# A chunked recurrence with a soft mixture of experts: Grams one step earlier, a new order of all instructions, and stores in half columns

## The chip, the cores and the metric

The kernel runs on one core of a Trainium2 chip. The metric is the time of one execution in device microseconds, the median of three runs. A core has five instruction streams that the profile names PE (TensorE; its weight loads have a row of their own, PEld), DVE (VectorE), ACT (ScalarE), POOL (GpSimd) and SP (SyncE, which here issues the data transfers). Everything is float32, but for the last products in fp32r.

## The reference

For 4 batches and 8 heads a state of 40 x 40 runs through 768 steps; then 3072 tokens of 320 values go through a soft mixture of 8 experts with 4 slots each.

```
for t in range(768):
    y[t]  = r[t] @ state
    Sa    = state @ a[t]
    state = state * w[t] - outer(Sa, b[t]) + outer(v[t], k[t])
x = y, as 3072 tokens x 320
logits = x @ phi                                   # 3072 x 32 slots
d = softmax(logits over tokens);  slot_in = d.T @ x
slot_out[e] = relu(slot_in[e] @ w1[e]) @ w2[e]     # 320 -> 1024 -> 320
out = softmax(logits over slots) @ slot_out
```

## The kernel before

The 768 steps are cut into 12 stages of 64, and a stage into two halves of 32 (q = 0, 1). The 8 heads of one batch go in groups of 3, 3 and 2 (120, 120 and 80 channels), times 4 batches: 12 groups.

For every stage there is work that does not depend on the state: running products of the decay w (scan_s, scan_k, scan_c: scans of 128 x 390 on VectorE and the products with k, b and a), a block-diagonal form of a (bda_at, ScalarE), and four Grams (gram, one for each batch): the products of k and b with a, 128 x 512 in one PSUM bank. Of a Gram, two 32-row parts go to the triangular systems (lls, two copies), and the rest is multiplied by a mask into SBUF (mls, VectorE). The systems of two stages are solved together (solve_in, 30 pairs of products and sums in solve_step on VectorE or GpSimd, solve_out): each of those steps needs the one before.

The chain is what the state runs through, stage by stage and half by half: chain_v (the part of v, 32 products of 32 x 40 columns, from mls), chain_a (the part of the state), chain_e (a copy to SBUF), chain_u (U, 32 products with the solved systems), six copies of U, and chain_s (the new state). Between these stand the output of the stage before (y_ut, y_sd, y_p, y_y), the transposes for later stages (kbtok, ctok_of) and the slots' online softmax (slots_a to slots_e). After the last stage come W1 (first), W2 (so), the combination of the slots' results (sr, s4) and the output: 24 products of 128 x 320, each copied from PSUM, and 12 stores of 256 x 320.

The program first records all operations (Plan.record) and only then issues them (Plan.emit). What comes when is written out in three strings: ORDER has two characters for each operation and is the order of the whole program, so each engine gets its own subsequence; ENGINE chooses ScalarE or VectorE for the copies marked `either`, and VectorE or GpSimd for the steps marked `both`; BANKS chooses a PSUM bank for every tenancy. Engines wait on each other by semaphores for data, and PACE holds transfers back when too many bytes are under way. All operations are issued from one helper line, L912 in the profile.

The order in which operations are recorded (the numbers in ORDER count them) is given by the loop over the stages, which records the Grams of stage st + 3 and the preparation of stage st + 4 behind the chain of stage st. The lines to which the change refers most:

```
nc.vector.tensor_tensor(mls[st][b][0:96], gr[0:96], mask_g[0:96]..., ALU.mult)
up = [bank(f"ups{st}"), bank(f"upt{st}")]
grams(st + 3)
run(*solve_items(st // 2 + 1))
nc.sync.dma_start(out[r].rearrange("(k p) c -> p k c", p=128), o2)
```

Of the kernel before, what the change touches and what calls it, by code (L numbers as in the profile page):

```python
# [14 lines left out]
MEM = 5560  # L15

B, H, S, D = 4, 8, 768, 40
C = 64
# [22 lines left out]
    "%:%9&,%k%p%n%l&R'[#,&O%m%o']'_%r%?%;%q&<&W&2%s%t%v'`'a'b'c'd%u&L&6&>%x&;&X&[%w&*%y&$%z%}%{&Y&%&.(N&#(L%|&Z&]"
    "&^&M&_&N&`(M&a&c&d'e'f&z'g'h&b'i'j'k&e&f&|'''l&9&g'm'%(O&A'n&='.'o&?&B&{'p&h&i&l&o&j&m&k&}'q'r&@'J's&D't'O&G"
    "'L'#&y'&(F(J'$'('F'u'D(G(K&s'v'w'x&C&n'K'y'z&H'{'+'-&v','/(H&p(I&F&t')&E&u'*'G&K(q&q'E&J(o(u&w(w'M(r(n(p(s)%"
    ")'(}&I&x)()&'8'9':(v'|'}(#($(%(&&r'@'B(''N(('Q'4()'R'T(x'5(y'U(t(*'6)^'S'<'7'A'H)_(z'V*`*f'^(+(,(-(.(/(0'X*c"
    "'P*6'C(1(2'?*a(3*4(|*b)$'Y'I(P';(4(5(6*d(7(8(9(:*7*e(Q*g*h)Y'W)))5(;(<(S)1)-'=)Z'>*j*5(=)*)T(>*k(?(A(D(B(C(@"
    "*l*i(T*m(R)7)6)3)/(E).)2(X*n)+)=(U(V(W(Z([*{)4(Y({(]*t*u*|)0)>(^(b'Z)9)U(`(_)[)8+#(a(d)#):);),(h+$+%+&(k(c*p"
    ")W(e+'+(+)(i)<)V+*(l(j(m)X*+(f(g)])`)a)b)c++)d)f)h)e)g)j+,+-+.)S*q)?)@*}*r)B*))A)i)C)E*%)k+/*#+f+l)l)D+g+0+n"
    ")m+1+2**+3)G+e*&*$*'+4+5)K)p+j)J+6)q)s)F+7+8)o*L)H*,)r*(*-+9)I)O)Q)P)N)R*N)n*O*.)w)L*Q*M)z*J+m+h)M*K*T){+k*D"
    "*E+:*P)|+;+<+i*8*R+=*U*/*1*3)}*S*@*B*0*X+o,3)x)y,5,9*2,;+>,4,6,7*W*<+?+@+A+B+C*A*C*H+D*V+E*Z*:*>,<*Y-U*]*G)t"
    "+F,:,=+G,8,o)u)v*I*s*;*[*F-S,X,]*9,Y+H,>.$.*,y+I+J.'+K+L+M+N+O,^,t.%+P+Q+R+S+T+U.&-V*=.(+p.)+q+V+W+X+Y+Z+[+]"  # L50
    "+^.+.,*^-T+s,L,N,Z,T,H..+_,M*?+`,z,P+t,[,U./*o,V,J,I.0+w,R,Q+v.A+u+x+r,C,B,?,@,A+z.B.-.C+{+y.D+|,F,O.1,}.:+}"
    ",2-$-#,K.E,W,&,{,u,$,%,#,),G,,.F,(.2.G,',w*_,|,/,v,S.H,_,D,x-D.3.I.J,*.K,-,+,0.9,.,1-%-B-'-(-H,E-J-.-+-,-&-)"
    "-E.L.M.N.O-*-/.P,a,`+b,e--.Q,b.R,p.S+c+a,d,q-0-C-I.T.U,s-F,c-1+d,f,g,i##,k-2-4.V.W.X.Y-6,h-7.5.;/f-K-l-L-3-5"
    "/.,j.6-G.Z.7/h.[-o-8-n-O.]/g-;-p-N-m,r.^-P._.`-M,m-Q,n-R/i->///4-s,l-t-h/,/--A-i-9-d/2-[.a-</5.b.c-q/3-j/0-W"
    "-g-^-e-=/1-f/S-:.d-r.e/T-u-k/V.f-v.g.h/].i.j.k.l-Y/U-x/W/Z/X-w-?-z0u-y/[0w0x-@-`0v0C.m-X/^.4/_0A/z-{-_-].n.o"
    ".p.q0#.r.s/Y-Z-b.#0D/`1G1D.t1J-a.u/|.v-}-|1E1H/61F.8/7.w.x1I-c.y.z/v.{.|.}/#/$/}/%/r/&/{/9/:1K/80$/a0&0B/<1L"
    "/;/x/t/w/=/b0(/c/>/A/@/s/n1N/+1O/)/(/'0+/y/B/C/*/j/?1P/u0%0;1M/p1Z1Q/D/E0?*v/G/k/q/l/e/F0'/o1b/I0E/P/M0@0)/m"
    "/H0=/J0>1U0<1c1R/N1e1f1g/K0f/Q1S/R/d/L1h1i1j1k1l1m0d/O0j0F1n0G0H0I0g0l1V0O0J0M0e0h0K1o0L0N0*1W0P0,0/0Q0-1p1Y"
    "1q1r1s0k08050607090m0i010R0n0S2N1t0.0X000U0V0T1415121u0W170]1T2L2O0`131v2J0o1w2K162H1[180Y0:3)2I1x2M0^1y0_3'"
    "2P3*3(1z0r0a1{0b0q0p0t1;2s2Q5<2y1>1<1|1}2#2w0c5=3A1=0s2q2t101?2x2r0304021@1&0y1*112u0Z1'0{0[0}1)1(1+4-1:1,0|"  # L60
    "1d1C1B1#2$2%2&2'2(2)2*2+1A2,2z1-2v2{1X5K3?4+192|45424/2-4.2.2/20212223241.3@370z40412p43443=1/463+3947333/2G"
    "4,3>3T2R25262728292S1%2:2;.<3B2<2=2}2>3-381]1$352?34313U302@2A2B492C4:2D2E3,2U3;4;2F4L4M4N2V4<3<3R483#2Y2Z2W"
    "2X2T3$2^2[3P2]3S524=3&3.4O4P4Q2_4R2`4S3:2d2c4>2b4T2f4D4U4V4W3L4X2a2j2e2m3N3Q2g534?4Y3C3M3O3u4Z4E4[3w2n4]4^5F"
    "2h323J4_4`4a3}2o3{2k2l2i3%4b3V3W3Y3X5P4c364d3Z3v3_3^3]3x3y3[4e3`5G3b5U3H3c3|5Y4f3a4g4h4i4j5Q3d3h3f3g3e3j3i3G"
    "4F4k3z4#4l4m3K3I4n4o5H555W4p4q574$3q3n4r4s4t4u5V4v4@4w4x4y4z4{5R5S3F4|3E3D3k4}3o5?5Z5M56545>3l5T4%5#5L5X3t5["
    "4'4&4(4*5z5{5$5|3m5}3r6%3p5N5O7*5I5:6'6&5;585%5&5'5(5)5*5+5,5-5J3s4)6#5^6(6$5.5/505]645@7+5_6)515`655b6*6`6c"
# [293 lines left out]
def rwkv_softmoe(ctx, tc, kb, aa, ww, rr, vv, vt, consts, phi, w1, w2, out):  # L360
# [8 lines left out]
    cs_t = cst.tile([128, 419], F32, name="cs_t")
    mask_g = cs_t[:, 0:64]  # L370
    mask_p = cs_t[:, 64:128]
    ident = cs_t[:, 128:256]
    sel, jj = cs_t[:, 259:291], cs_t[:, 291:419]
# [835 lines left out]
```

## Time and profile before

| | us |
|---|---|
| median of 3 runs (lowest, highest) | 381.95 (381.11, 383.08) |
| the profiled execution | 381.42 |
| its span | 379.7 |
| PE busy, PEld busy | 320.9, 280.4 |
| DVE busy | 304.7 |
| ACT busy | 211.5 |
| POOL busy | 114.8 |

Mean granted TensorE clock over the span: 0.936 of full speed. Data moved: 162 GB/s over the span.

The span is from the first instruction to the last, and the time of the execution has 1.7 us around it. Busy times of different engines overlap, so they do not add up; which of them holds up the end differs from stretch to stretch. An fp32 product appears as two matmul rows and two load rows, so counts in the trace are twice those in the code.

### The profile page before, as it was taken

The page shows a single profiled execution, that of the slowest core. Times are in us where ns is not written, and L with a number is a line of the kernel's source. Part 1 is how long each engine was busy: PE and PEld are TensorE (multiplying, and loading weights), DVE is VectorE, ACT ScalarE, POOL GpSimd, SP SyncE. Part 2 cuts the span into 40 slices and gives each one's busy share as a digit, 9 for nine tenths or more (in the row PEclk, how much of TensorE's full clock was granted, in tenths as well). Part 3 has the DMA queues.
Part 4 walks back from the last instruction along what each step waited for, and adds up shares of the span by engine and source line. Part 5 has one row for each costly group of instructions (what it writes and reads, how often), then busy time and mean ns, then how long its engine had stood idle before and what let it go on. Part 6 is the DMA issues. An engine that isn't in the chain of part 4 may idle for free.

```text
span 379.7 us, 15848 instructions
## 1 busy us (share of the span) xinstructions
PE 320.9 (85%) x6889; PEld 280.4 (74%) x6889; DVE 304.7 (80%) x660; ACT 211.5 (56%) x490; POOL 114.8 (30%) x220
## 2 busy tenths in 40 slices
...
GB/s 260 303 241 154 36 13 254 38 101 79 105 194 102 154 57 198 179 40 60 196 129 133 156 154 177 250 234 225 154 245 174 236 137 214 214 283 279 3 124 294
DMA packets 32798, 62.45 MB, mean 164 GB/s; under 512 B 3768, under 2 KB 18232, under 8 KB 32728
## 3 DMA queue, kind: packets, MB, share of 16 engines
...
q8 instruction: 54, 0.88, 1.0%
...
HBM read 57.49 MB, written 3.93 MB: 162 GB/s over the span
## 4 chain that ended last, share of the span: by engine, by line
PE 70%; DVE 10%; ACT 7%; issue 7%; DMA 1%; POOL 0%; ACTq 0%; DVEq 0%; POOLq 0%
PE ps L912 70%; DVE wt L912 7%; ACT wt L912 6%; DVE ps L912 1%; DVE mem L912 1%; DMA wt<-in_kb_dram 1%; ACT old L912 1%; ACT mid L912 0%; ACT mem L912 0%; ACT old_r L912 0%; POOL wt L912 0%; DVE slx L912 0%; DVE sls L912 0%; DVE mid L912 0%; ACTq L1205 0%
## 5 line engine op out<-in xcount | busy, mean ns | idle before, releaser
L912 PE MATMUL ps<-wt,wt 96*32 96x40 f32 (+7 forms) x2872 | 147.2, 240 | 14.8 <-ACT wt L912 7.2
L912 PEld LDWEIGHTS ps<-wt,wt 96*32 96x32 f32 (+7 forms) x2872 | 135.0, 134 | 22.8 <-issue 10.0
L912 POOL TENSOR_TENSOR wt<-wt 128x130 f32<-128x130 f32 (+14 forms) x194 | 96.1, 496 | 98.7 <-DVE wt L912 65.0
L912 ACT COPY wt<-ps 128x320 f32<-128x320 f32 (+3 forms) x120 | 53.5, 478 | 70.0 <-PE ps L912 56.8
L912 ACT ACTIVATE wt<-ps 32x256 f32<-32x256 f32 (+1 forms) x168 | 66.9, 399 | 27.8 <-PE ps L912 21.0
L912 PE MATMUL ps<-wt,mem 128*64 128x40 f32 (+4 forms) x1056 | 79.4, 264 | 2.3 <-issue 2.3
L912 PEld LDWEIGHTS ps<-wt,mem 128*64 128x64 f32 (+4 forms) x1056 | 67.3, 125 | 8.3 <-issue 2.7
L912 PE MATMUL ps<-wt 32*32 32x40 f32 (+2 forms) x1824 | 66.7, 223 | 4.1 <-DVE wt L912 2.0
L912 PE MATMUL ps<-cs_t,wt 120*128 120x120 f32 (+4 forms) x352 | 50.0, 279 | 22.8 <-ACT wt L912 10.7
L912 PEld LDWEIGHTS ps<-wt 32*32 32x32 f32 (+2 forms) x1824 | 54.2, 117 | 9.2 <-ACT wt L912 4.4
L912 PEld LDWEIGHTS ps<-cs_t,wt 120*128 120x128 f32 (+4 forms) x352 | 38.8, 148 | 27.4 <-issue 12.8
L912 DVE TENSOR_TENSOR wt<-wt 128x150 f32<-128x150 f32 (+14 forms) x166 | 55.4, 334 | 4.1
L912 DVE TENSOR_TENSOR wt<-ps,cs_t 96x512 f32<-96x512 f32 (+1 forms) x72 | 48.1, 683 | 4.9 <-PE ps L912 4.5
L912 DVE TENSOR_TENSOR_SCAN ps<-wt,wt 128x390 f32<-128x390 f32 x48 | 45.6, 977 | 0.9 <-ACT mem L912 0.2
L912 DVE TENSOR_TENSOR wt<-wt,ps 128x6 f32<-128x6 f32 (+2 forms) x72 | 37.4, 549 | 0.1
L912 ACT ACTIVATE wt<-wt,bm_t 128x768 f32<-128x768 f32 (+1 forms) x36 | 29.9, 863 | 4.2 <-PE ps L912 1.8
L912 DVE TENSOR_TENSOR ps<-ps,wt 120x480 f32<-120x480 f32 (+1 forms) x30 | 17.6, 602 | 15.3 <-PE ps L912 15.3
L912 ACT COPY mem<-ps 120x480 f32<-120x480 f32 (+3 forms) x48 | 21.4, 446 | 7.4 <-PE ps L912 5.3
L912 DVE STREAM_TRANSPOSE wt<-wt 128x1024 f32<-128x1024 f32 x12 | 24.8, 2080 | 0.6 <-ACT wt L912 0.5
L912 ACT ACTIVATE mid<-ps 64x320 f32<-64x320 f32 x42 | 18.1, 430 | 7.4 <-PE ps L912 5.5
L912 POOL TENSOR_SCALAR_AFFINE_SELECT wt<-wt 128x1024 f32<-128x1024 f32 x6 | 7.6, 1264 | 45.5 <-DVE wt L912 45.5
L912 DVE TENSOR_TENSOR wt<-ps,wt 120x480 f32<-120x480 f32 (+1 forms) x33 | 19.1, 593 | 1.5 <-PE ps L912 1.0
...
## 6 DMA issues: line engine op xcount, KB each, us to landing
...
wt<-in_kb_dram SPq DMA_DIRECT2D x24, 384.0 KB
...
mem<-in_vt_dram SPq DMA_DIRECT2D x12, 384.0 KB
mem<-in_rr_dram SPq DMA_DIRECT2D x12, 384.0 KB
...
```

What stands on the lines that cost most here:

```text
L912: nc.gpsimd.memset(t, 0.0)
```

## The change

1. Grams are recorded and ordered four stages ahead of the chain, not three, and the solve steps of a pair of stages likewise one pair earlier, with solve_out apart from them. A fourth set of mls tiles holds the Grams of the further stage.
2. chain_v multiplies 32 rows, not 96, in a stage's first half, where the rows from 32 on meet only zeros.
3. U of a half-stage goes to one PSUM bank, not two; the two 64-row copies into ub become one of 128 rows.
4. The mask is applied to 64 rows of a Gram, and the rows 64 to 95 (columns 32 to 63 of each head) are copied by a further instruction on ScalarE or VectorE.
5. The output is made for 160 columns at a time: the first half's products, copies and 8 stores (128 x 3 x 160) are recorded before the second half of W2. There are 16 groups of 3 products of 160 columns in place of 24 of 320.
6. Smaller edits: constants of 227 columns, not 419; some small tiles moved or shared; a memset of the vu tiles is gone; PACE's third number is 240e3.
7. ORDER, ENGINE and BANKS are new throughout.

```diff
-PACE = (40, 500e3, 256e3, 1400e3)
+PACE = (40, 500e3, 240e3, 1400e3)
...
-        mls = Ring([hct(t) for t in mls[4 * i:4 * i + 4]] for i in range(3))
+        mls = Ring([hct(t) for t in mls[4 * i:4 * i + 4]] for i in range(4))
+        gss = Ring([space(HD)])
+        pcs = Ring(space(NG) for _ in range(6))
+        pms = Ring(space(3 * NG).rearrange("p (g j) -> p g j", j=3) for _ in range(2))
+        sit = gss.tiles[0][:, 0:3 * NSL].rearrange("p (k s) -> p k s", k=3)
         lgs = Ring([space(128)])
-        ex, dd = space(128), space(128)
-        mg_t = space(160)
+        ex = dd = space(128)
+        mg_t, jj = sdt[:, 0:160], sdt[:, 160:288]
...
-            nc.vector.tensor_tensor(mls[st][b][0:96], gr[0:96], mask_g[0:96].unsqueeze(1).broadcast_to([96, H, C]), ALU.mult)
+            ml = mls[st][b]
+            nc.vector.tensor_tensor(ml[0:64], gr[0:64], mask_p[0:64].unsqueeze(1).broadcast_to([64, H, C]), ALU.mult)
+            nc.either.copy(ml[64:96, :, 32:64], gr[64:96, :, 32:64])
...
+            n = 96 if q else 32
...
-                    nc.tensor.matmul(gp[r, h * D:(h + 1) * D], mls[st][b][0:96, h, 32 * q:32 * q + 32], vu[0:96, head(b, h)],
+                    nc.tensor.matmul(gp[r, h * D:(h + 1) * D], mls[st][b][0:n, h, 32 * q:32 * q + 32], vu[0:n, head(b, h)],
...
-            up = [bank(f"ups{st}"), bank(f"upt{st}")]
+            up = bank(f"ups{st}")
             nc.gather = True
             for h in range(H):
                 for b in range(B):
                     r = slice(32 * b, 32 * b + 32)
-                    nc.tensor.matmul(up[b // 2][r, h * D:(h + 1) * D], tt[r, c, h, :], gs[r, h * D:(h + 1) * D],
+                    nc.tensor.matmul(up[r, h * D:(h + 1) * D], tt[r, c, h, :], gs[r, h * D:(h + 1) * D],
                                      start=True, stop=True)
             nc.gather = False
             ur = slice(64 + 32 * q, 96 + 32 * q)
             for b in range(B):
-                nc.either.copy(vu[ur, b * HD:b * HD + HD], up[b // 2][32 * b:32 * b + 32, 0:HD], scale=-1.0)
-            ub = ubs[q][:, 0:HD]
-            for i in range(2):
-                r = slice(64 * i, 64 * i + 64)
-                nc.either.copy(ub[r], up[i][r, 0:HD], scale=-1.0)
+                nc.either.copy(vu[ur, b * HD:b * HD + HD], up[32 * b:32 * b + 32, 0:HD], scale=-1.0)
+            nc.either.copy(ubs[q][:, 0:HD], up[:, 0:HD], scale=-1.0)
...
-        run(*solve_items(0))
+        solve(0)
+        solve_out(0)
...
+        grams(3)
+        solve(1)
...
-                grams(3)
                 load_w(4)
                 load_k(4)
                 prep(4)
                 bda_at(4)
+                grams(4)
...
-                    grams(st + 3)
                     kbtoks(st + 3)
                 if st + 4 < NST:
                     prep(st + 4)
                     bda_at(st + 4)
+                    grams(st + 4)
...
-                run(*solve_items(st // 2 + 1))
+                solve_out(st // 2 + 1)
+            if st % 2 == 1 and st // 2 + 2 < NSS:
+                solve(st // 2 + 2)
...
-        nc.scalar.copy(s4[:, HC * hf:HC * hf + HC], sr[:, 0:HC])
-    heads = 2 * C * (NSS - 1)
-    n = 0
-    for j in range(S // 256):
-        for b in range(B):
-            r = slice(b * S + 256 * j, b * S + 256 * j + 256)
-            o2 = wts[n // 8][:, 2 * HD * (n % 8):2 * HD * (n % 8) + 2 * HD].rearrange("p (k c) -> p k c", k=2)
-            for k in range(2):
-                t = 256 * j + 128 * k
+        cols = slice(HC * hf, HC * hf + HC)
+        nc.scalar.copy(s4[:, cols], sr[:, 0:HC])
+        for n in range(2 * B):
+            b, g = divmod(n, 2)
+            x = 8 * hf + n
+            o3 = wts[x // 10][:, 3 * HC * (x % 10):3 * HC * (x % 10) + 3 * HC]
+            op = bank("pt_a")
+            for k in range(3):
+                t = 128 * (3 * g + k)
                 src = cst_old[:, heads * b + t:heads * b + t + 128] if t < heads else rnd[0][:, 128 * b:128 * b + 128]
-                op = bank("pt_a")
-                nc.tensor.matmul(op[:, 0:HD], src, s4, start=True, stop=True)
-                nc.either.copy(o2[:, k], op[:, 0:HD])
-            nc.sync.dma_start(out[r].rearrange("(k p) c -> p k c", p=128), o2)
-            n += 1
+                nc.tensor.matmul(op[:, HC * k:HC * k + HC], src, s4[:, cols], start=True, stop=True)
+            nc.either.copy(o3, op[:, 0:3 * HC])
+            r = slice(b * S + 384 * g, b * S + 384 * g + 384)
+            nc.sync.dma_start(out[r].rearrange("(k p) c -> p k c", p=128)[:, :, cols], o3.rearrange("p (k c) -> p k c", k=3))
```

Three places of the order follow. In them ps_61 to ps_68 are the eight PSUM banks, the other names SBUF tiles, and the shape is that of the result for one instruction.

TensorE, the second half of stage 6 in the chain, before: a product of the slots, chain_v (32 products), a Gram, chain_u (32 products in two banks), a Gram.

```order
L912 MATMUL ps_65<-mid,phs 32x128 x4
L912 MATMUL ps_64<-wt_76,wt_73 32x40 x2
L912 MATMUL ps_64<-wt_76,wt_71 32x40 x2
...
L912 MATMUL ps_68<-wt_71,wt_70 128x192 x2
L912 MATMUL ps_68<-wt_71,wt_70 128x128
L912 MATMUL ps_62<-wt_74 32x40 x2
L912 MATMUL ps_64<-wt_74 32x40 x2
...
L912 MATMUL ps_66<-wt_71,wt_70 128x192 x2
```

After, the same half of stage 6: transposes, chain_v, then y_y (22 products of 64 rows), chain_u in one bank, and transposes.

```order
L508 MATMUL ps_61<-cs_t,wt_70 128x80 x4
L508 MATMUL ps_62<-wt_76,wt_77 32x40 x2
L508 MATMUL ps_62<-wt_76,wt_74 32x40 x2
...
L508 MATMUL ps_67<-mem 64x120 x4
L508 MATMUL ps_67<-mem 64x80 x2
L508 MATMUL ps_67<-wt_75,wt_77 64x40
L508 MATMUL ps_67<-wt_75,mem 64x40
...
L508 MATMUL ps_63<-mem,wt_74 32x40 x32
L508 MATMUL ps_68<-cs_t,wt_70 128x120 x4
```

Between V and U there is now an output product in place of a Gram of three products, and behind U transposes.

VectorE, the end of the first solve, before: the last solve steps, two Gram masks, solve_out (the STREAM_TRANSPOSE into wt_74) and the scan for stage 4 behind it.

```order
L912 TENSOR_TENSOR wt_72<-wt_72 128x27x4
L912 TENSOR_TENSOR wt_72<-wt_72 128x84
L912 TENSOR_TENSOR wt_72<-wt_72 128x28x3
L912 TENSOR_TENSOR wt_72<-wt_72 128x58
L912 TENSOR_TENSOR mem<-ps_65,cs_t 96x512
L912 TENSOR_TENSOR wt_77<-ps_64,cs_t 96x512
L912 STREAM_TRANSPOSE wt_74<-wt_72 128x32x32
...
L912 TENSOR_SCALAR wt_76<-ps_64 32x320
```

After: a scan of stage 4 (SCALAR_TENSOR_TENSOR 128x390), its product of 128x384 and a mask of 64 rows (into mem, of stage 3) stand among the solve steps, and solve_out closes them.

```order
L508 TENSOR_TENSOR wt_72<-wt_72,wt_70 128x13x18
L508 SCALAR_TENSOR_TENSOR ps_68<-wt_70,wt_71 128x390
L508 TENSOR_TENSOR wt_70<-wt_72 128x238
L508 TENSOR_TENSOR mem<-ps_66,cs_t 64x512
L508 TENSOR_TENSOR wt_73<-wt_73,ps_68 128x384
L508 TENSOR_TENSOR wt_70<-wt_72 128x240
L508 TENSOR_TENSOR wt_72<-wt_72,wt_70 128x15x16
...
L508 TENSOR_TENSOR wt_70<-wt_72 128x30
L508 TENSOR_TENSOR wt_72<-wt_72,wt_70 128x30
L508 STREAM_TRANSPOSE wt_74<-wt_72 128x32x32
```

Before solve_out there are 107 instructions on VectorE before the change and 120 after it.

TensorE at the end, before: the last products of W2 (32x160), four transposes for the token weights, the two combinations of the slots (sr), and the first of 24 output products.

```order
L912 MATMUL ps_67<-wt_76,mem 32x160 x2
L912 MATMUL ps_67<-wt_77,mem 32x160 x2
L912 MATMUL ps_63<-cs_t,mem 128x128 x4
L912 MATMUL ps_62<-mid_r_5148,mid_r_5146 128x160 x2
L912 MATMUL ps_64<-mid_r_5147,mid_r_5146 128x160 x2
L912 MATMUL ps_68<-mid_r_5149,mid_r_5145 128x320
L912 MATMUL ps_65<-mid_r_5149,old_r_5071 128x320
```

After: the combination of the first half, six groups of three output products, the second half of W2, two more groups, the second combination, and the groups of the second half.

```order
L508 MATMUL ps_66<-mid_r_5195,mid_r_5194 128x160 x2
L508 MATMUL ps_67<-mid_r_5197,old_r_5086 128x160 x2
...
L508 MATMUL ps_68<-mid_r_5197,old_r_5086 128x160 x3
L508 MATMUL ps_63<-wt_74,mem 32x160 x2
L508 MATMUL ps_63<-wt_75,mem 32x160 x2
L508 MATMUL ps_63<-wt_74,mem 32x160 x2
...
L508 MATMUL ps_63<-wt_77,mem 32x160 x2
L508 MATMUL ps_65<-mid_r_5197,old_r_5086 128x160 x3
L508 MATMUL ps_67<-mid_r_5197,old_r_5086 128x160 x3
L508 MATMUL ps_64<-mid_r_5196,mid_r_5194 128x160 x2
L508 MATMUL ps_61<-mid_r_5197,old_r_5086 128x160 x3
```

The output products of the first half now stand before and behind the second half of W2, and only eight groups behind the second combination.

## Rows read from the trace of the kernel before

**Rows 1.** The page, busy us (share) xinstructions of each engine, whole span
```profile
PE 320.9 (85%) x6889; PEld 280.4 (74%) x6889; DVE 304.7 (80%) x660; ACT 211.5 (56%) x490; POOL 114.8 (30%) x220
```

**Rows 2.** The page, chain that ended last, shares by engine
```profile
PE 70%; DVE 10%; ACT 7%; issue 7%; DMA 1%; POOL 0%; ACTq 0%; DVEq 0%; POOLq 0%
```

**Rows 3.** Stretches: length, busy us of PE, PEld, DVE, ACT, POOL, clock, DMA share, GB/s
```profile
10.17:58.57 48.40, 33.59 (x233) 29.54 (x234) 46.87 (x97) 32.78 (x71) 10.08 (x20) 0.86 0.50 154
58.57:70.00 11.43, 8.42 (x289) 7.58 (x290) 9.24 (x15) 4.66 (x11) 6.00 (x14) 0.71 0.51 158
70.00:156.00 86.00, 83.34 (x1991) 76.23 (x1991) 82.26 (x166) 62.02 (x142) 36.97 (x68) 1.00 0.40 121
...
369.36:379.70 10.34, 0.00 (x1) 0.00 (x0) 0.50 (x2) 1.34 (x5) 0.00 (x0) 0.64 0.84 298
```

**Rows 4.** Waits of TensorE: cause, us in total, times, longest
```profile
PE ps L912 <- issue: 18.5, 15, 3.0
PE ps L912 <- ACT wt L912: 17.9, 11, 10.2
PE ps L912 <- DVE wt L912: 8.3, 4, 5.6
```

**Rows 5.** Timeline of TensorE: start, duration, instructions, [wait before <-cause]
```profile
58.57 0.37 PE L912 MATMUL ps<-wt 32*32 32x40 f32 x9 [1.49 <-DVE wt L912]
...
161.63 0.45 PE L912 MATMUL ps<-cs_t,wt 120*120 120x120 f32 x1 [2.99 <-issue]
...
304.14 0.27 PE L912 MATMUL ps<-wt,mem 96*32 96x40 f32 x1 [2.33 <-issue]
```

**Rows 6.** Stretches between fetch waits, and two behind them
```profile
156.68:161.63 4.95, 1.95 (x128) 1.62 (x128) 3.16 (x6) 2.57 (x6) 2.67 (x9) 0.90 0.65 206
273.74:278.29 4.55, 3.30 (x128) 2.73 (x128) 4.35 (x12) 1.59 (x4) 1.27 (x2) 1.00 0.96 255
...
161.63:168.40 6.77, 6.77 (x41) 6.61 (x43) 2.44 (x5) 1.68 (x4) 1.78 (x5) 0.57 0.12 42
304.14:310.90 6.76, 6.75 (x50) 6.27 (x50) 2.18 (x4) 1.12 (x3) 0.00 (x0) 0.50 0.53 172
```

**Rows 7.** The page, DMA queues: packets, MB, share of 16 engines
```profile
q8 instruction: 54, 0.88, 1.0%
```

**Rows 8.** Groups by form: xcount, busy us, mean ns, idle before
```profile
L912 DVE TENSOR_TENSOR_SCAN ps<-wt,wt 128x390 f32<-128x390 f32 x48 | 45.6, 977 | 0.9 <-ACT mem L912 0.2
...
L912 ACT ACTIVATE wt<-ps 32x256 f32<-32x256 f32 x92 | 34.5, 376 | 8.1 <-PE ps L912 6.0 <-DVE wt L912 0.2
...
L912 ACT ACTIVATE wt<-ps 32x320 f32<-32x320 f32 x76 | 32.4, 427 | 19.7 <-PE ps L912 15.0 <-DVE wt L912 3.0 <-issue 0.5
L912 DVE TENSOR_TENSOR wt<-ps,cs_t 96x512 f32<-96x512 f32 x40 | 26.5, 682 | 1.2 <-PE ps L912 1.0
...
L912 DVE TENSOR_TENSOR wt<-wt,ps 128x768 f32<-128x768 f32 x24 | 22.2, 947 | 0.0
...
L912 PE MATMUL ps<-wt,wt 96*32 96x40 f32 x1280 | 21.6, 209 | 6.7 <-issue 4.1 <-ACT wt L912 2.4
L912 PE MATMUL ps<-wt 32*32 32x40 f32 x1536 | 21.4, 207 | 4.1 <-DVE wt L912 2.0 <-issue 1.7
...
L912 ACT ACTIVATE mid<-ps 64x320 f32<-64x320 f32 x42 | 18.1, 430 | 7.4 <-PE ps L912 5.5 <-DVE wt L912 1.3
...
L912 ACT COPY wt<-ps 128x480 f32<-128x480 f32 x24 | 13.4, 562 | 5.2 <-PE ps L912 5.1
...
L912 DVE TENSOR_TENSOR wt<-wt,ps 128x384 f32<-128x384 f32 x24 | 12.7, 545 | 0.0
```

**Rows 9.** Timeline of the store queue: start, us, instructions
```profile
365.97 9.86 SPq L912 DMA_DIRECT2D out_dram<-wt  x12
```

**Rows 10.** Stretches of the tail, columns as in rows 3
```profile
366.50:378.00 11.50, 2.86 (x16) 1.97 (x14) 3.14 (x8) 4.20 (x13) 0.00 (x0) 0.75 0.96 342
...
358.82:363.20 4.38, 4.38 (x132) 3.95 (x125) 1.52 (x3) 0.29 (x1) 0.00 (x0) 1.00 0.01 4
```

More of the change, by code (lines that the diff above doesn't have):

```diff
@@ L14 @@
 PSUM = bass.MemoryType.PSUM
-MEM = 5560
+MEM = 5736
 B, H, S, D = 4, 8, 768, 40
@@ L41 @@
[L41 to L60, printed above, removed]
@@ L76 @@
[L76 removed]
+    "#+#/#6#0#-#,#.#1#3#5#4#(#2#$#&#*#%#8#7#:#9#;#=#A#<#?$m#@#B#>#'#F#C$q#E#W#D#X#G#H#I#J#K#M#L#Y$s#[#]$t#Z#i#l#_"
@@ L367, in rwkv_softmoe @@
     bank = nc.bank
[L369 to L373, printed above, removed]
+    cs_t = cst.tile([128, 227], F32, name="cs_t")
+    ident = cs_t[:, 0:128]
+    sel = cs_t[:, 131:163]
+    mask_p = cs_t[:, 163:227]
     wts = [cst.tile([128, 5 * FF], F32, name=f"wt{i}") for i in range(8)]
@@ L400, in rwkv_softmoe @@
     mlast = cst.tile([128, 1], F32, name="mlast")
-    sit = cst.tile([128, 3, NSL], F32, name="sit")
     slm, cst_t, stk = {}, {}, []
@@ L458, in rwkv_softmoe @@
         lt_a, n_a = (ht(part(2, 1024)) for _ in range(2))
-        tmp_r = [part(2, n) for n in (240, 240, 240, 240)]
+        tmp_r = [part(0, 240) for _ in range(2)]
         cps = Ring(part(3, 768) for _ in range(2))
-        mls = [part(i, 512) for i in (3, 3, 1, 1, 4, 4, 4, 4, 7, 7)]
+        mls = [part(i, 512) for i in (3, 3, 1, 1, 1, 2, 2, 4, 7, 7, 4, 4, 4, 4)]
         ahs = Ring(gc(part(i, 768)) for i in (4, 4, 3, 3, 3))
         tts = Ring([cht(part(4, 1024))])
-        gss = Ring([part(4, HD)])
         kbks = Ring(part(5, 1280) for _ in range(4))
@@ L472, in rwkv_softmoe @@
         ubt = part(7, 768).rearrange("p (u b t) -> p u b t", u=3, b=B)
-        pcs = Ring(part(4, NG) for _ in range(6))
-        pms = Ring(part(4, 3 * NG).rearrange("p (g j) -> p g j", j=3) for _ in range(2))
         bds = {}
@@ L815, in slots_c @@
             nc.tensor.transpose(tp[:, 0:128], ex, ident)
-            nc.scalar.copy(dd, tp[:, 0:128])
-            dds[i] = dd
             es = ess_t.put(i)
@@ L820, in slots_c @@
             ess[i] = es
+            nc.scalar.copy(dd, tp[:, 0:128])
+            dds[i] = dd
         def slots_e(i):
@@ L875, in merge_m @@
             mg["m"] = m
+            nc.scalar.copy(jj.rearrange("p (q s) -> p q s", q=4), sel.unsqueeze(1).broadcast_to([128, 4, NSL]))
             tp = bank("mg_m")
@@ L902, in merge_s, with solve @@
             nc.vector.tensor_copy(sit, tp[:, 0:96].rearrange("p (k s) -> p k s", k=3))
-        def solve_items(ss):
-            return ([lambda: solve_in(ss)]
-                    + [lambda i=i: solve_step(ss, i) for i in range(1, 31)] + [lambda: solve_out(ss)])
+        def solve(ss):
+            solve_in(ss)
+            for i in range(1, 31):
+                solve_step(ss, i)
         nc.vector.memset(one, 0.0)
```

70 lines of the change are left out of this document (42 added, 28 removed).

## The prediction

> **What bounds the kernel now.** I read the busy shares first, then the stretches of the span, then what TensorE waits for, and last the order of its instructions. TensorE (the PE rows) is busy 320.9 of 379.7 us, VectorE (DVE) 304.7, ScalarE (ACT) 211.5 [rows 1], and 70% of the chain that ended last is TensorE's own work, 7% is "issue", a wait that no other engine ended [rows 2]. The average hides four parts [rows 3]. From 10.17 to 58.57 us VectorE is busy 46.87 of 48.40 us and TensorE 33.59: the prologue waits for VectorE. From 70 to 156 us, and in most of what follows up to the tail, it is TensorE: busy 83.34 of 86.00 us. There it sets the pace, and what other engines do is hidden. After 369.36 us TensorE has nothing left and only the stores run, 10.34 us.
>
> TensorE's waits name three causes [rows 4]: "issue", 18.5 us in 15 waits; ScalarE, 17.9 us, of which one wait (the start) is 10.2; VectorE, 8.3 us in 4. The "issue" waits are the ones with no partner. Two of them are 2.99 us before 161.63 and 2.33 us before 304.14 [rows 5]. Between the end of such a wait and the instruction at which the one before began lie 128 matmuls and 128 weight loads, 256 instructions: in the piece from 156.68 to 161.63 TensorE works 1.95 us of 4.95, in that from 273.74 to 278.29 3.30 of 4.55 [rows 6]. The instruction queue moved 0.88 MB in 54 packets [rows 7], 16 KB each. I read this as TensorE running out of instructions: it gets them in pieces of 256, and a piece whose matmuls are short is used up before the next has come. In the list of packets the next piece comes on average 3.9 us after the piece before it was opened (2.6 to 5.7), so a piece with less work than that must wait; this delay is longest where the data queues are full, as with a DMA share of 0.96 in the second piece [rows 6].
>
> **Order, the fetch waits.** I cut TensorE's order list of both kernels into pieces of 256 (an fp32 matmul is two matmul rows and two loads) and priced each from the durations in the trace. Before, 6 pieces hold less than 2.5 us of work and their mean wait is 1.4 us; 11 hold 2.5 to 3.5 (mean wait 0.45), 8 hold 3.5 to 4.5 (0.45), the other 24 more (0.05): 8.4 + 5.0 + 3.6 + 1.2 = 18.2 us, which is the 18.5 of [rows 4]. Afterwards the counts are 2, 7, 14 and 27: 2.8 + 3.2 + 6.3 + 1.4 = 13.7 us, a gain of 4.5. The reason is what stands between the short matmuls: U and V are 32 matmuls each with 40 columns (0.2 us each [rows 8], but overlapping), and where before only a Gram stood between them, there is now an output product of 22 matmuls or a group of transposes. Measured by the work that is lacking to 4.5 us per piece, the sum falls from 31 to 18 us, by 42%, which would be 7.6 of 18.2. I take 5.5. Bounds: all 18.5 gone at one end; at the other +1, if the delay follows the data traffic and the traffic falls on other pieces.
>
> [...]
>
> **Clock.** [...] I take -2 of the 6.3; bounds -6.3, and +3 if a new long wait arises.
>
> **Prologue: Grams four steps ahead.** All that VectorE must do before solve 0 is out now includes stage 4's preparation and four more Gram masks: 107 instructions before, 120 after. Added are 4 scans of 0.977, 2 products of 0.947 and 2 of 0.545, and 4 masks of 0.682 [rows 8]: 3.9 + 1.9 + 1.1 + 2.7 = 9.6 us, some 0.6 of small ones, less about 1.5 since VectorE has one solve step fewer and shorter ones: 8.7 us. As VectorE has no slack there [rows 3], the first U product, which starts at 58.57 us after a wait for it [rows 5], moves to about 67. TensorE does nearly the same work before it in both (some 23 us). The work is not extra: it was done later. From 58.57 to 70 us TensorE is busy 8.42 of 11.43 us [rows 3], so 3.0 us of waits there can be filled by what is ready earlier, and the clock of 0.71 there leaves about as much again. I take 8.7 - 3.0 - 1.7 = +4. Bounds 0 and +8.7.
>
> **Copies and masks: hidden.** ScalarE: 52 more Gram copies of 0.376, 42 U copies of 0.430 gone, 23 new ones of 128 rows (taken at 0.43, since 32 and 64 rows take that too) and 11 more of 0.427 of 32 rows [rows 8]: 19.6 - 18.1 + 9.9 + 4.7 = 16.1, with the output copies +17 us on 211.5. It is busy 62.02 of 86.00 us in the TensorE-bound stretch [rows 3], and 17 us spread over 300 raise that from 72 to 78%. VectorE loses about 10 us (U copies and solve steps). The mask over 64 rows costs what it did over 96, 0.682: its time goes with its 512 columns. V with K=32: the row of K=96 has 209 ns for a matmul and that of K=32 207 [rows 8], so 32 matmuls in each of 12 stages give nothing. One bank for U: all 32 matmuls end before any copy in either version; the copies then read one bank in place of two, which no row shows. I set these to 0, with bounds -3 (fewer semaphore steps) and +4 (one copy of 0.4 us more ahead of a U step in half of 24 places).
>
> **Stores.** Now 12 stores follow the last product, from 365.97 us [rows 9], 3.93 MB at 342 GB/s with the queues 0.96 full [rows 10], 11.5 us. After, the eight stores of the first half (1.97 MB, 5.8 us) start while the second half's W2 product (4.38 us [rows 10]) runs, and only 5.8 us lie behind. That gains 5.8, less what the product is late by: between its matmuls TensorE now waits for output copies (ScalarE does 13 of 16, 0.56 us each [rows 8]), up to 3.7 us. So -5.8 + 3.7 = about -2. A row of a store is 640 bytes in place of 1280: if each piece took as long as now, the second half would need 11.5 us, and the term were +3.7. Bounds -5.8 and +3.7.
>
> **Sum.** 381.42 us of the profiled execution (span 379.7 and 1.7 around it) - 5.5 - 2 + 4 + 0 - 2 = 375.9. The median of the runs is 0.53 above the profiled one: 376.4 us.
>
> **Rivals.**
> 1. The prologue decides (slower). Nothing of the 8.7 us is regained, and TensorE, idle longer before the first U, starts it at the low clock as behind the 2.99 us wait (2.9 us): 376.4 + 4.7 + 2.9 = 384.0. For it: VectorE's 97% there, and two waits of TensorE for it. Against it: the work is only moved, and VectorE is freed by it later. It decides from the point where the first U starts after 66 us and TensorE's work at 100 us is still 8 behind.
> 2. The fetch waits stay as they are, since the delay is set by the traffic: 381.95 + 4 - 2 = 383.9 with the clock as now. For it: the longest ones lie where DMA is at 0.65 to 0.96 [rows 6]. Against it: pieces with over 4.5 us of work hardly ever wait. [...]
> 3. The waits and the clock drops nearly go: -12 and -5 in place of -5.5 and -2, 366.9 us. For it: the largest waits are the ones in the shortest pieces, and there are 2 of these left. Against it: the stores that feed the later pieces, and 14 pieces near the limit.
>
> **Chances.** Forecast 0.55 (its own range 371 to 381), rival 1 0.16, rival 2 0.15, rival 3 0.14. The range reaches from 367 (rival 3) to 385 (rivals 1 and 2 with a little beyond). A measurement here tells about 0.5%, 1.9 us, from no change. Faster than 380.0: 0.50 of the forecast and all of rival 3, 0.64. Within: 0.04 + 0.06 + 0.08 = 0.18. Slower than 383.9: 0.01 + 0.10 + 0.07 = 0.18.
>
> **What would show it.** "issue" waits of TensorE of 12 to 14 us, none of 2 us or more in a piece that now holds over 3.5 us of work; the first U at 65 to 68 us; fewer than 10 us of low clock after 70 us; first stores starting before the last W2 product ends, and 9 to 11 us from that product's end to the end of the span plus what it was late. It is wrong if "issue" is 17 us or more, if TensorE waits for ScalarE or VectorE in the stretch from 100 to 300 us by more than 5 us, or if the stores of 640 bytes run at well under 342 GB/s.

## The result, and the profile after

The changed kernel takes 371.95 us (median of 4 runs, 369.64 to 373.7) against 382.12 us of the kernel before (4 runs): a ratio of 0.973, with a 95% interval of 0.966 to 0.980. Medians here and below are over all runs of a group, ratios and intervals only over the runs within 1.5% of the fastest of their kernel, so a ratio need not be the quotient of two medians. The forecast was 376.4 us with a range of 367 to 385. The profiled execution took 369.64 us, its span is 367.9 us; it is the fastest of the four and lies 2.3 us under the median. Terms below are differences between this span and the 379.7 us of before.

The busy shares, from the page of the changed kernel, answer to [rows 1]: TensorE 3.2 us less (320.9 before), VectorE 9.7 us less, ScalarE 15.0 us more.

```profile
PE 317.7 (86%) x6913; PEld 279.1 (76%) x6913; DVE 295.0 (80%) x630; ACT 226.5 (62%) x527; POOL 112.7 (31%) x228
```

Its waits of TensorE (cause, us in total, times, longest) answer to [rows 4]:

```profile
PE ps L508 <- ACT wt L508: 22.0, 12, 9.8
PE ps L508 <- issue: 8.0, 6, 2.4
PE ps L508 <- DVE wt L508: 8.0, 6, 5.1
```

"issue" has fallen from 18.5 to 8.0 us, ScalarE's part has risen by 4.1 us, VectorE's is nearly the same. Stretches (length, busy us of PE, PEld, DVE, ACT, POOL, clock, DMA share, GB/s) answer to [rows 3]:

```profile
9.79:66.37 56.58, 35.98 (x244) 31.62 (x245) 54.80 (x110) 42.64 (x93) 10.45 (x19) 0.80 0.53 172
66.37:70.00 3.63, 3.63 (x94) 3.32 (x98) 3.63 (x4) 2.18 (x6) 0.07 (x1) 0.50 0.00 0
70.00:156.00 86.00, 84.63 (x2134) 76.94 (x2127) 83.05 (x166) 64.78 (x151) 37.17 (x77) 1.00 0.41 122
```

The prologue is longer: up to the first U product VectorE is busy 54.80 of 56.58 us, and the clock in the first microseconds behind it is 0.50. From 70 to 156 us TensorE is busy 84.63 of 86.00 us (83.34 before). The first 100 us as one stretch, before and after:

```profile
0.00:100.00 100.00, 71.97 (x1225) 65.00 (x1226) 91.80 (x180) 60.80 (x131) 34.88 (x66) 0.90 0.47 145
```

```profile
0.00:100.00 100.00, 69.09 (x1100) 61.81 (x1104) 92.82 (x189) 71.37 (x158) 27.47 (x53) 0.86 0.45 141
```

The first U product, in the timeline of TensorE:

```profile
66.37 0.37 PE L508 MATMUL ps<-mem,wt 32*32 32x40 f32 x9 [1.79 <-DVE wt L508]
```

It starts at 66.37 us (58.57 before, [rows 5]). The remaining waits named issue, from the timeline of TensorE:

```profile
200.96 0.25 PE L508 MATMUL ps<-wt,mem 128*64 128x40 f32 x1 [1.26 <-issue]
...
253.66 0.26 PE L508 MATMUL ps<-cs_t,wt 120*120 120x120 f32 x1 [2.38 <-issue]
...
266.98 0.41 PE L508 MATMUL ps<-wt,wt 96*32 96x40 f32 x21 [0.93 <-issue]
...
271.63 0.20 PE L508 MATMUL ps<-wt,wt 128*64 128x40 f32 x1 [1.08 <-issue]
...
295.44 0.41 PE L508 MATMUL ps<-mid,phs 128*32 128x128 f32 x5 [2.15 <-issue]
```

The sixth is 0.21 us long, at 109.42 us. Each stands at a multiple of 256 instructions in TensorE's order; between the third and the fourth of these there are 127 matmuls in the record and 128 loads (first row of the next fence). The pieces before them hold, by the price list of the prediction, 3.40, 2.05, 3.73, 3.25 and 1.55 us of work: the two pieces under 2.5 us have the two waits over 2 us. The price list runs lower than the busy rows: 3.25 us against 3.56 us for the fourth piece, the first row of the next fence. Stretches of the same kernel, that piece, the stores of the second half, and the low clock behind the two longest waits:

```profile
266.98:271.62 4.64, 3.56 (x127) 3.18 (x128) 1.27 (x3) 2.68 (x7) 2.55 (x4) 1.00 0.87 254
361.00:366.50 5.50, 0.00 (x0) 0.00 (x0) 0.00 (x0) 0.60 (x2) 0.00 (x0) 0.78 0.96 291
254.85:258.26 3.41, 3.41 (x20) 3.41 (x19) 1.32 (x2) 1.90 (x5) 1.17 (x3) 0.50 0.26 91
295.81:299.22 3.41, 3.41 (x19) 3.27 (x18) 0.61 (x2) 0.79 (x2) 0.00 (x0) 0.50 0.93 227
```

Behind the waits of 2.38 and 2.15 us the clock is at its low level, 0.50, for 3.41 us each, so each cost 1.7 us of TensorE work; before, it was 2.9 and 3.4 [rows 6]. These two are all the low clock between 100 us and TensorE's last product. Before the change there were three such stretches between 100 us and the last product:

```profile
160.69:167.52 6.83, 5.89 (x32) 5.89 (x33) 1.89 (x3) 1.68 (x4) 2.56 (x7) 0.50 0.19 60
259.67:263.08 3.41, 3.41 (x78) 1.98 (x77) 2.37 (x5) 2.05 (x6) 1.06 (x3) 0.50 0.85 284
300.63:310.87 10.24, 7.91 (x112) 7.27 (x104) 4.47 (x12) 3.14 (x8) 0.00 (x0) 0.50 0.67 204
```

The stores, in the timeline of the store queue, and the two halves of W2 in that of TensorE:

```profile
350.86 13.54 SPq L508 DMA_DIRECT2D out_dram<-wt  x16
```

```profile
343.39 4.55 PE L508 MATMUL ps<-wt,mem 128*32 128x160 f32 x128
...
351.61 4.55 PE L508 MATMUL ps<-wt,mem 128*32 128x160 f32 x128
```

From the first W2 product to the end are 367.90 - 343.39 = 24.51 us; before they were 379.70 - 354.37 = 25.33 (the product's start read from its timeline). The first stores are issued before the second half of W2 begins. Groups by form (xcount | busy us, mean ns | idle before), for [rows 8]:

```profile
L508 DVE TENSOR_TENSOR wt<-ps,cs_t 64x512 f32<-64x512 f32 x42 | 27.7, 675 | 0.6 <-ACT wt L508 0.3
...
L508 PE MATMUL ps<-wt,wt 96*32 96x40 f32 x672 | 10.6, 209 | 1.1 <-issue 0.9
...
L508 ACT COPY wt<-ps 32x256 f32<-32x256 f32 x42 | 15.0, 362 | 1.2 <-DVE wt L508 0.4
...
L508 PE MATMUL ps<-wt,wt 32*32 32x40 f32 x672 | 9.9, 205 | 1.8 <-ACT wt L508 1.5 <-DVE wt L508 0.3
```

The mask over 64 rows takes 675 ns (682 over 96). V over 32 rows has 205 ns, over 96 rows 209. The 48 new copies of Gram rows are the COPY row: 42 there at 362 ns.

### The profile page after: what moved, and what is told of

Read it like the earlier page. It is cut to its first block, busy times and chain, and to the rows that moved or that the text cites. A ratio compares the mean times of both kernels' runs of the same rounds, so it can differ in the third digit from the quotient of the medians.

```text
span 367.9 us, 15907 instructions
## 1 busy us (share of the span) xinstructions
PE 317.7 (86%) x6913; PEld 279.1 (76%) x6913; DVE 295.0 (80%) x630; ACT 226.5 (62%) x527; POOL 112.7 (31%) x228
## 5 line engine op out<-in xcount | busy, mean ns | idle before, releaser
L508 PE MATMUL ps<-wt,wt 96*32 96x40 f32 (+8 forms) x2936 | 146.1, 238 | 13.8 <-ACT wt L508 10.1
L508 PEld LDWEIGHTS ps<-wt,wt 96*32 96x32 f32 (+8 forms) x2936 | 133.9, 133 | 22.3 <-ACT wt L508 11.7
L508 PE MATMUL ps<-wt,mem 128*32 128x160 f32 (+7 forms) x1088 | 85.9, 295 | 1.8 <-issue 1.3
L508 PEld LDWEIGHTS ps<-wt,mem 128*32 128x32 f32 (+6 forms) x1088 | 67.0, 123 | 12.9 <-issue 8.3
L508 ACT COPY wt<-ps 32x256 f32<-32x256 f32 (+4 forms) x133 | 58.6, 465 | 26.1 <-PE ps L508 16.5
L508 POOL TENSOR_TENSOR wt<-wt,wt 128x58 f32<-128x58 f32 (+14 forms) x108 | 52.9, 490 | 61.8 <-DVE wt L508 44.3
L508 POOL TENSOR_TENSOR wt<-wt 128x150 f32<-128x150 f32 (+14 forms) x96 | 43.5, 453 | 44.1 <-DVE wt L508 27.3
L508 PEld LDWEIGHTS ps<-cs_t,wt 120*128 120x128 f32 (+4 forms) x352 | 37.5, 146 | 22.2 <-ACT wt L508 12.9
L508 DVE TENSOR_TENSOR wt<-ps,cs_t 64x512 f32<-64x512 f32 (+1 forms) x74 | 48.7, 677 | 5.1 <-PE ps L508 4.5
L508 PE MATMUL ps<-wt 120*64 120x192 f32 (+1 forms) x288 | 46.2, 311 | 0.0
L508 PEld LDWEIGHTS ps<-wt 120*64 120x64 f32 (+1 forms) x288 | 36.2, 136 | 0.0
```

The lines of the kernel that those rows point to most:

```text
L508: eng.dma_start(dst, src)
```

## The experiments

Ratios are to the kernel before, timed beside each group on the same chip; the kernel before gave 381.3, 382.0 and 381.8 us in the three groups, with runs from 374 to 391, so a difference under 2 us between medians of 6 to 13 runs says little. A profile is one execution.

**The changed kernel again, and its borders moved.** The theory to be tested is that the issue waits are waits for pieces of 256 instructions, and that the work in each piece decides. The edit adds only tiny products where TensorE is idle (56 for shift224 in place of 20), so the same work in the same order is cut at other places:

```diff
-FILLS = {}
+FILLS = {163: (20, 7, 0)}
...
-            self.nc.tensor.matmul(bank, src, src, start=True, stop=True)
+            r = slice(32 * (_ % 4), 32 * (_ % 4) + 32)
+            self.nc.tensor.matmul(bank[r, 0:8], src[r, 0:32], src[r, 0:8], start=True, stop=True)
...
-        nc.idle = (ex, ident, sys._getframe().f_lineno)
+        nc.idle = (one, ident, sys._getframe().f_lineno)
```

Expected of the changed kernel itself, of shift80 and of shift224:

> The changed kernel itself, as the base of this group: 372 us, 'issue' waits of TensorE about 8 us. Both theories expect the same.

> The changed kernel with 20 tiny products (80 instructions) put ahead of TensorE's first instruction, where TensorE is idle for 9.8 us anyway, so that every later border between pieces of 256 instructions lies 80 instructions earlier in the program. Theory 1 (the waits named issue come where a piece of 256 holds too little work): the work that pieces lack to 4.5 us rises from 17.8 to 26.5 us, so the issue waits go from 8 to 12 or 13 us, at other places of the program, and the time to 376 to 377 us. Theory 2 (the order of the work took the waits away, wherever the borders lie): nothing moves, 371 to 373 us, issue waits 8 us at the same products.

> The same with 56 tiny products (224 instructions). Theory 1: the work lacking to 4.5 us falls from 17.8 to 13.4 us and that lacking to 3.5 us from 5.2 to 2.3, so the issue waits go from 8 to 5 us and the time to 369 to 370 us. Theory 2: 371 to 373 us.

Measured: 371.74 us for the changed kernel (ratio 0.972, 0.963 to 0.981), 376.43 for shift80 (0.989, 0.984 to 0.994), 366.75 for shift224 (0.965, 0.958 to 0.972). One of shift80's 13 runs took 1012.93 us, for which nothing here gives a reason; the others lie between 372.57 and 384.33. Work that TensorE did in its idle time cost 4.7 us or gave back 5.0 by the medians, 6.4 or 2.6 by the ratios. The issue waits of the three profiled executions (the changed kernel's took 374.79 us, shift80's 384.33, shift224's 367.9), one row each:

```profile
PE ps L508 <- issue: 10.7, 6, 2.7
```

```profile
PE ps L509 <- issue: 15.2, 10, 4.4
```

```profile
PE ps L509 <- issue: 7.2, 7, 1.4
```

The order of the three is the one that theory 1 gives, and the sizes were 13, 8 and 5 us forecast against 15.2, 10.7 and 7.2. The waits moved as theory 1 says: in the changed kernel's first trace those after 100 us have 2735, 7065, 9609, 10119, 10373 and 11647 recorded matmuls and loads of TensorE ahead of them, and in shift80 five of the ten have the same counts (2735, 7065, 9609, 10373, 11647), though 80 of these are now the tiny products. Theory 2 falls. The interval of shift80 lies clear of that of the changed kernel; that of shift224 overlaps with it (0.963 to 0.972), and so do its six runs (362.25 to 367.9) with the lowest of the changed kernel's (365.19 to 374.79). Its median lies under the 369 to 370 us that theory 1 asked for, and its 7.2 us of waits within what unmoved borders give (6.0 to 10.7 us, see the end of this section). What shift224's trace lacks is the long waits: none is over 1.4 us, against 2.4 and 2.7 for the longest of the changed kernel, and between 100 and 345 us its clock is low for 3.4 us, against 6.8 and 13.7. That the gain lies there is argued, not shown by a run of its own. Nor does the tiny work change what comes after it in the prologue. From 10 to 100 us in the second trace of the changed kernel, in shift80 and in shift224:

```profile
10.00:100.00 90.00, 68.57 (x1068) 61.57 (x1069) 85.75 (x175) 69.23 (x155) 23.45 (x45) 0.83 0.42 129
```

```profile
10.00:100.00 90.00, 68.75 (x1052) 61.59 (x1053) 85.07 (x172) 69.13 (x155) 23.40 (x45) 0.83 0.41 128
```

```profile
10.00:100.00 90.00, 68.14 (x1062) 61.33 (x1063) 85.59 (x174) 69.13 (x155) 23.39 (x45) 0.83 0.42 131
```

The trace of shift80 is that of the slowest of its ordinary runs, 8 us over its median. Two stretches of it:

```profile
303.00:307.24 4.24, 0.00 (x0) 0.00 (x0) 0.00 (x0) 2.21 (x6) 0.00 (x0) 0.94 0.99 283
253.82:258.48 4.66, 2.86 (x127) 2.57 (x128) 2.54 (x8) 3.90 (x10) 1.80 (x6) 1.00 0.82 254
```

The second is a piece with 127 recorded matmuls that does 2.86 us of work in 4.66. The first lies in front of the longest wait, 4.41 us: TensorE does nothing in it, and the data queues are at 0.99. No other issue wait in the traces here is over 4 us.

**The old order with its borders moved.** The same edit with 56 products in the kernel before.

> The kernel before with the borders of the pieces 224 instructions earlier in the program (56 tiny products in TensorE's idle start). Theory 1 (only the work in each piece counts): the work lacking to 4.5 us falls from 30.9 to 28.6 us, so the issue waits stay at 15 to 17 us and the time falls by 1 to 2 us, to 379.5 to 381 us: no border makes the old order good. Theory 2 (the changed kernel's gain was a lucky place of its borders): the old order gains as much as the changed one did, 5 us, to 376 to 377 us.

Measured: 383.13 us (ratio 0.999, 0.993 to 1.005), no change, with 15.4 us of issue waits in the profile. The gain of 5 us that theory 2 asked for is excluded; the 1 to 2 us of theory 1 were not seen either. So by the price list the old order has many short pieces wherever it is cut (the lack to 4.5 us lies between 28.6 and 35.7 us at all 16 places that I worked out, and between 13.4 and 26.5 us for the new one), and the changed kernel owes its gain to the order and not only to the place of the borders: cut at three places the new order takes 366.75 to 376.43 us, cut at two the old one takes 382 and 383 us. The place is worth 9.7 us between the two moved ones that were tried.

**Less data under way.** Does a piece come late because it queues behind data?

```diff
-PACE = (40, 500e3, 240e3, 1400e3)
+PACE = (40, 500e3, 240e3, 700e3)
```

> The changed kernel with at most 0.7 MB of large transfers under way in place of 1.4 (PACE's fourth number). Theory 1 (the next piece of instructions is late because it queues behind data packets): the issue waits fall from 8 to 11 us to 5 to 7, and the time by 2 to 4 us, to 368 to 370 us. Theory 2 (the delay of a piece is fixed, whatever the data queues hold): issue waits 8 to 11 us, 371 to 373 us. Theory 3: transfers come too late, TensorE waits for data more, 374 us or more.

Measured: 428.08 us (ratio 1.121, 1.117 to 1.125). Waits of TensorE:

```profile
PE ps L508 <- DMA mem<-in_vt_dram: 12.9, 2, 6.9
...
PE ps L508 <- DMA wt<-in_w_dram: 7.5, 3, 6.8
...
PE ps L508 <- issue: 4.0, 4, 1.6
```

The issue waits fell to 4.0 us, below what theory 1 asked for, but theory 3 decides the time: TensorE now waits for data, 12.9 us for v and 7.5 us for the experts' weights among others. As it uses its instructions more slowly then, the fall of the issue waits has two possible reasons, and the question stays open.

**The mask over 96 rows.** Does ScalarE's added work cost anything?

```diff
-            nc.vector.tensor_tensor(ml[0:64], gr[0:64], mask_p[0:64]..., ALU.mult)
-            nc.either.copy(ml[64:96, :, 32:64], gr[64:96, :, 32:64])
+            nc.vector.tensor_tensor(ml[0:96], gr[0:96], mask_g[0:96]..., ALU.mult)
```

> The changed kernel with the Gram mask over 96 rows again and without the 48 copies of rows 64 to 95 (ScalarE does nearly all of them, some 18 us of its time). Theory 1 (ScalarE's added work is hidden behind TensorE): 371 to 373 us, ScalarE's busy time 208 us in place of 226. Theory 2 (TensorE's 22 us of waits for ScalarE come in part from these copies): 368 to 370 us.

Measured: 369.54 us (ratio 0.970, 0.965 to 0.974) beside 371.74 of the changed kernel (0.972, 0.963 to 0.981). The page's busy row:

```profile
PE 316.1 (86%) x6913; PEld 277.8 (76%) x6913; DVE 294.3 (80%) x630; ACT 209.8 (57%) x479; POOL 113.1 (31%) x228
```

ScalarE is busy 16.7 us less than after the change, and the time moves by less than the intervals. The median lies in theory 2's range, but 2.2 us under the changed kernel is within the scatter, so the run excludes neither theory. TensorE's waits for ScalarE fall by 2.4 us in the trace, from 22.0 to 19.6, and those for VectorE rise from 8.0 to 12.7.

**V over 32 rows and U in one bank, in the old order.** One edit in chain_v, one in chain_u, and the second needs 13 other tenancies in other banks, since a U bank is then held longer:

```diff
+            n = 96 if q else 32
...
-                    nc.tensor.matmul(gp[...], mls[st][b][0:96, h, ...], vu[0:96, head(b, h)],
+                    nc.tensor.matmul(gp[...], mls[st][b][0:n, h, ...], vu[0:n, head(b, h)],
...
-            up = [bank(f"ups{st}"), bank(f"upt{st}")]
+            up = [bank(f"ups{st}")] * 2
```

> The kernel before with two edits alone: V of a stage's first half over 32 rows, and U in one bank (its two copies of 64 rows stay). Order of everything as before. Theory 1 (they are worth nothing): as the kernel before within 1 us, 381 to 383 us. Theory 2 (less to read and to wait for on the chain): 378 to 380 us.

> The kernel before with one edit: V of a stage's first half over 32 rows; banks and order as before. Theory 1 (the 11 us that both edits together cost lie in U's one bank, or in the 13 other tenancies that had to take other banks for it): 381 to 383 us. Theory 2 (they lie in the products over 32 rows): 388 to 393 us.

Measured: 393.16 us with both (ratio 1.032, 1.026 to 1.037), 381.91 us with V alone (1.006, 0.999 to 1.013). Both theories of the first run are wrong: the pair is 11 us slower. V over 32 rows shows no difference, as forecast. Waits of TensorE, with both edits and with V alone:

```profile
PE ps L912 <- ACT wt L912: 20.8, 19, 10.2
PE ps L912 <- DVE wt L912: 12.8, 9, 5.8
```

```profile
PE ps L913 <- ACT wt L913: 16.3, 11, 10.2
PE ps L913 <- issue: 13.4, 11, 3.2
PE ps L913 <- DVE wt L913: 7.7, 3, 5.5
```

With the bank edit there are 19 waits for ScalarE in place of 11 and 9 for VectorE in place of 3. Whether one bank for U does this, or the moved tenancies, was not taken apart. In the changed kernel the same one bank stands in an order and a placement made for it.

**The tail alone.** The changed kernel with the old tail, and the kernel before with the new one; the tails are exchanged whole, from the first product of W2's last stage on, with their order. Core of the edit of the first:

```diff
-                nc.tensor.matmul(op[:, HC * k:HC * k + HC], src, s4[:, cols], start=True, stop=True)
+                nc.tensor.matmul(op[:, 0:HD], src, s4, start=True, stop=True)
...
-            nc.sync.dma_start(out[r].rearrange("(k p) c -> p k c", p=128)[:, :, cols], ...)
+            nc.sync.dma_start(out[r].rearrange("(k p) c -> p k c", p=128), o2)
```

> The changed kernel with the tail of the kernel before: both halves of W2 first, 24 products of 320 columns, 12 stores of 256 x 320 in rows of 1280 bytes. Theory 1 (the half-column stores gain what the two traces differ by from the first W2 product to the end, 25.3 against 24.5 us): 372.5 to 373 us. Theory 2 (the forecast's term): 374 us. Theory 3 (stores with rows of 640 bytes are slower by so much that nothing is gained): 371 to 372 us.

> The kernel before with the tail of the changed one (half columns, 16 stores, the first eight ahead of the second half's W2). Theory 1 (the same 2 us that the changed kernel lost with the old tail): 379 to 380.5 us. Theory 2 (0.8 us, as between the two traces): 380.5 to 381.5 us. From the first W2 product to the end 23.5 to 24.5 us in place of 25.3.

> The kernel before with the tail of the changed one, now with PACE's third number at 240e3 too: a half-column store has 245,760 bytes, so under 256e3 it counted as a small transfer and only two were let under way at a time (the stores took 18.75 us from the first to the last issue). Theory 1 (that was the loss): from the first W2 product to the end 25 us or less in place of 29.5, and 379 to 382 us. Theory 2 (the half-column tail does not suit the old order, whatever the pace): 384 to 386 us again.

Measured: tail12 373.8 us (0.986, 0.980 to 0.991), 2.1 us over the changed kernel, as the forecast's term said; the two intervals just meet, so the size is uncertain. In its trace the products of W2, now both halves, begin at 345.69 us:

```profile
345.69 8.90 PE L507 MATMUL ps<-wt,mem 128*32 128x160 f32 x256
```

From there to the end of the span (372.2) are 26.5 us, 2.0 more than in the changed kernel. In the old order the first version took 385.7 us (1.007, 1.002 to 1.012), 3.7 us more than before, so both theories of before_tail16 missed. There a store of 245,760 bytes counted as small and only two were under way; with the changed PACE it took 381.69 us (1.000, 0.994 to 1.006). The store queues of the two:

```profile
358.88 18.75 SPq L911 DMA_DIRECT2D out_dram<-wt  x16
```

```profile
362.30 16.68 SPq L911 DMA_DIRECT2D out_dram<-wt  x16
```

It is 2.1 us shorter, but in the changed kernel it is 13.54 us. The two W2 products in the second of them:

```profile
354.29 4.55 PE L911 MATMUL ps<-wt,mem 128*32 128x160 f32 x128
...
364.32 6.78 PE L911 MATMUL ps<-wt,mem 128*32 128x160 f32 x128
```

They begin 10.03 us apart (8.22 in the changed kernel), and the second took 6.78 us; the granted clock from 364 to 377 us was 0.81 on average. From the first to the end of the span (382.9) it is 28.6 us, so theory 1 of the last run missed its 25 us, though the time lies in its range. The interval (0.994 to 1.006) overlaps that of the first version (1.002 to 1.012), so what PACE is worth here is not clear of the scatter.

**Two of these together.** Mask over 96 rows and borders moved by 224.

> The changed kernel with two of the earlier edits together: the mask over 96 rows without the 48 copies, and the borders of the pieces 224 instructions earlier in the program. Theory 1 (they act on different things, so they add): 364 to 366 us, issue waits 4 to 7 us. Theory 2 (the mask's 2 us were only scatter between runs): 366 to 368 us, as with the moved borders alone.

Measured: 365.37 us (ratio 0.965, 0.958 to 0.973; runs 362.55 to 367.81), the lowest median of all, 6.6 us under the changed kernel. It is not told apart from shift224 alone (366.75), so whether the two add is not shown. But beside the mask over 96 rows alone (369.54 us, 368.28 to 372.69) all its six runs are faster: the moved borders gain 4.2 us there too. Its issue waits:

```profile
PE ps L508 <- issue: 7.5, 8, 1.4
```

**How far one trace can be trusted.** Four traces have the new order with its borders unmoved up to the tail: the changed kernel's two (8.0 and 10.7 us of issue waits), mask96 and tail12, in this order here:

```profile
PE ps L507 <- issue: 6.0, 5, 2.7
```

```profile
PE ps L507 <- issue: 9.4, 8, 2.3
```

Four have the old order: the kernel before (18.5), k32_alone (13.4), before_tail16 and tail16_paced:

```profile
PE ps L911 <- issue: 15.2, 16, 3.3
```

```profile
PE ps L911 <- issue: 16.9, 13, 3.5
```

The means are 8.5 and 16.0 us. The two ranges do not meet, so the fall is real, but on average it is 7.5 us and not the 10.5 that the first pair of traces gives. The low clock between 100 and 345 us scatters as well: 6.8 to 13.7 us in the four new traces, 10.2 to 20.5 in the old ones. The sum of the waits is not all that counts: mask96_shift224 has more of them than mask96 (7.5 and 6.0 us) and is faster, and its longest is 1.4 us in place of 2.7.

## Why the prediction was right, and where its sizes were off

The way, the sign and the range were right: 371.95 us lies 4.5 us under the forecast, and the gain was 10.2 us where about 5.6 was forecast. By steps, in us of span, from the first pair of traces:

| step | forecast | measured | read from |
|---|---|---|---|
| fetch waits | -5.5 | -10.5 | 18.5 to 8.0, waits of TensorE |
| clock | -2 | -5.2 | stretches of low clock after 100 us |
| prologue | +4 | +2.9 to +4.4 | TensorE's busy time up to 100 us; its work done by the price list |
| copies, masks, K=32, one bank | 0 | 0 to -1.6 | the rest; mask96, k32_alone |
| stores | -2 | -0.8 | first W2 product to the end |

The sum of the measured is -13.6 to -12.1 against -11.8 of the spans; two waits, of 0.7 and 1.2 us, lay ahead of 100 us and are in two lines, and without them it is -11.7 to -10.2.

- **Fetch waits: the mechanism right, the term too small.** The two shortest pieces waited 4.5 us, where 2.8 was forecast. But the 14 pieces with 3.5 to 4.5 us of work, for which 6.3 us was charged at the old mean of 0.45, waited 0.9 us in all. The mean of that band did not carry over. The other estimate of the prediction, the lack to 4.5 us (7.6), was nearer, and it is close to the 7.5 us that the means of four traces give, so part of the miss is the scatter of one pair. shift80 and shift224 showed that the cut matters. Where one wait follows another a piece later, the rows give the time from opening a piece to the start of the next: 4.95 and 4.55 us before [rows 6], 4.64 after and 4.66 in shift80, all above the mean of 3.9 that the prediction read from the list of packets, which no row shows (in the trace of before, the instruction packet behind a border landed 2.4 us after it on average, and the 14 waits at borders ended 1.3 to 1.6 us after a landing). Nor is this time longest where the data queues are fullest, as the prediction says: of the two pieces in [rows 6], the one with a DMA share of 0.65 took 4.95 us and the one with 0.96 took 4.55.
- **Clock: right in kind, too small.** The stretches of low clock between 100 us and the last product, three before and two after, begin between 0.9 us ahead of and 1.3 us behind the end of a wait of 1.0 to 3.0 us. Half of TensorE's busy time in them is 8.6 and 3.4 us. No run shows the -2 of the forecast: it was the author's choice out of 6.3 us (6.77 x 0.43 and 6.76 x 0.50 [rows 6]), and the first pair of traces shows -5.2 in its place. A long wait does not always bring one: in the kernel before, a wait of 2.15 us ended at 229.53 us, and the clock stayed at 1.00 from there to 240 us.
- **Prologue: as worked out.** The first U came at 66.37 us against "about 67" forecast, and by 100 us 3.4 to 4.9 of the 7.8 us were regained, so rival 1, which asked for 8 us left at 100 us, is out. TensorE's work ahead of it is 33.59 us of busy time before [rows 3] and 35.98 after, not the "some 23" of the prediction, but nearly the same in both, as it held. No run took this term apart.
- **Hidden copies: right.** ScalarE's 15 us more show only in 4.1 us of waits for it, none of which lies between 100 and 300 us, where the prediction said that more than 5 us would prove it wrong. Taking 16.7 us away again moved the time by no more than the intervals. One bank for U was bounded at +4 us; in the old order that edit, with its moved tenancies, cost 11. No bound from the rows held this, since the rows showed no tenancy that waits.
- **Stores: right in kind, too large in the trace.** Of the 5.8 us, 3.7 went to the second W2 product, which starts at 351.61 rather than at the end of the first (347.9). The 3.7 us are the forecast's number, but by luck: it stood for waits for output copies, and in the trace TensorE waits there once, 0.38 us, and else does the transposes, the combination and the six groups of output products put between the halves. The stores of 640-byte rows then ran at 291 GB/s, not at 342 [rows 10], so 1.97 MB took 6.8 us in place of 5.8: 5.8 - 3.7 - 1.0 = 1.1. By medians (tail12) it was 2.1. Stores well under 342 GB/s were one of the prediction's signs of being wrong; at 291 that sign came, and it cost this term 1.0 us.
- **Rival 3 had two terms nearer.** It put -12 and -5 on the waits and the clock, at a chance of 0.14, where the first pair of traces shows -10.5 and -5.2. Its total of 366.9 us was still further off than the forecast's.
- **Rival 2.** The waits did not stay as they were, so rival 2 is out. Before the change 14 of the 15 issue waits, 17.8 of 18.5 us, stood a multiple of 256 records of TensorE apart, and 80 instructions ahead of the program's first product cost 4.7 us, so in this kernel such places cost time.
